# Storing the falling tiles by way of device memory, and another order in the last pair of an attention and Fourier-mixing kernel

## The chip, the cores and the metric

The kernel runs on one core of a Trainium2 chip. The core has a matrix engine (TensorE, PE in the profile), a vector engine (VectorE, DVE), a scalar engine (ScalarE, ACT), a general engine (GpSimd, POOL) and a fifth that here only issues transfers (SyncE, SP). Each runs its own list of instructions in order and waits on semaphores for the others. Transfers between device memory and the core's on-chip memory (SBUF) are carried by 16 DMA engines, called lanes here. SyncE or ScalarE issues a transfer; its pieces then queue in the lanes, and each lane that takes part reports its landing on a semaphore.

The metric is the device time of one execution, in microseconds (us). Three executions of the kernel before took 1045.64, 1046.65 and 1047.59 us; the median is 1046.65.

## The reference

There are 4 batches of 768 tokens, 8 heads of 64 columns. First comes block-sparse attention, with a mask over blocks of 32 tokens, then a Fourier mixing layer with a two-layer network:

```python
scores = where(mask, q @ k.T / 8, -1e9)
x = softmax(scores) @ v                 # 4 x 768 x 512 after the heads are joined
u = x + real(fft2(x))                   # along tokens and along columns
un = (u - mean(u)) / sqrt(var(u) + 1e-6)
out = u + relu(un @ w_ch1) @ w_ch2      # 512 -> 2048 -> 512
```

All inputs and the output are float32.

## The kernel before

The attention of the four batches runs in 96 slots of some 6 to 8 us. A slot computes scores for two tiles of keys (`scores`, L583), exponentials on ScalarE (`weigh`, L603 and L611), the mask on VectorE (L613) and products with v (`values`, L657). Beside the attention of batch b, the kernel carries out the mixing of batch b-1 in the gaps that a planner inside the program finds with estimated costs. The order of the instructions on every engine is fixed when the program is built. After the last slot only the mixing of batch 3 is left, from some 790 us on.

A batch's 768 tokens do not lie in SBUF in their order in memory. The Fourier transform along the tokens is folded by symmetries, and so the 768 rows are kept in six tiles of 128 partitions, three in `xA` (tiles 0, 1, 2) and three in `xB` (tiles 3, 4, 5). The table `_ORDER` says which rows a tile holds, as (tile, first partition, runs, jump, count, first row, step). Tiles 0, 1 and 5 rise: partition after partition holds every second row upwards. In tiles 2, 3 and 4 the partitions 1 to 126 hold rows that fall by two, as two interleaved runs (tile 2: 382, 380, ... and 383, 381, ...), and partitions 0 and 127 hold a row each apart.

`_rows` turns this table into transfers. A rising tile is stored by two transfers of 64 rows (tile 5 by four). A falling tile is stored by three: one row, then 2 x 63 rows in one transfer whose outermost dimension has size 2, then one row. `store` (L1289) issues them, all on SyncE except where the caller names ScalarE. Stores of batches 0, 1 and 2 are called from `channels` (L1279) once the last quarter of the second layer has been added to x (L1284).

The buffers `xA` and `xB` exist twice. The attention output of batch b is therefore copied (`place`, L681, on ScalarE) into the buffer that batch b-2 is stored from, and must wait until those stores have read it. Copies of pair 0 of batches 2 and 3 are placed after the program has emitted batch b-2's stores for that half (`until`).

Between the normalisation and the first layer, rows and columns of `un` must be swapped. For batches 0, 1 and 2 VectorE transposes blocks of 32 x 32 in place (L1019), SyncE writes the tile to device memory (`far<-un`, L1020), and when all three tiles of a half have landed, SyncE gathers them back with the blocks in swapped order (`unT<-far`, four transfers, L1032). All this stands in SyncE's one list, together with the loads of the next pairs' q, k and v (`qb`, `kb`, `vr`) and the output rows of the attention (`row<-oT`, `x<-row`).

In batch 3 the second layer is done by `outputs` (L1335) as seven block products for each pair of tiles (m of xA and m of xB): seven products of four accumulating steps (L1349) take the place of eight, with sums and differences on VectorE (L1356, L1379, L1332). The pairs come in the order `OUT`, 0, 1, 2. After the last pair, tiles 2 and 5, nothing is left but their stores. They are issued by halves of 256 columns: `ends` marks the pair. The last thing stored is the right half of falling tile 2.

At the end of the program there is a branch over a general path that is taken only for large inputs, and closing waits for all transfers.

Of the kernel before, what the change touches and what calls it, by code (L numbers as in the profile page):

```python
# [11 lines left out]
FP32 = mybir.dt.float32  # L12
# [5 lines left out]
ALU = mybir.AluOpType  # L18
# [22 lines left out]
def _grid(ap, start, runs, jump, n, step):  # L41
# [17 lines left out]


_TURNED = (((0, 0, (128, 64, 2), (64, 128, 2), (1, 1, 64)),
# [39 lines left out]
def kernel(  # L101
# [14 lines left out]
    nc = tc.nc  # L116

    B, H, S, D = q.shape
    DM = H * D
    FF = w_ch1.shape[1]  # L120
    P = 128
# [9 lines left out]
    T = C // 2  # L131
# [55 lines left out]
    far_p = ctx.enter_context(tc.tile_pool(name="far_p", bufs=1, space=bass.MemoryType.DRAM))  # L187
    ps_s = ctx.enter_context(tc.tile_pool(name="ps_s", bufs=2, space=PSUM))
# [793 lines left out]
    z_at = [0.0, 0.0]  # L982
    rstd_at = deque()
    finished = set()
    folded = set()

    def mixer(b, xA, xB):
# [298 lines left out]
            if r == NF // 4 - 1:  # L1286
                store(half, m)

        def store(half, m, cols=slice(0, DM), queue=nc.sync):  # L1289
            x = (xA, xB)[half]  # L1290
            for p0, cnt, rows in _rows(out[b][:, cols], T * half + m):
                queue.dma_start(out=rows, in_=x[p0:p0 + cnt, m, cols])
            if cols.stop == DM:
                stored[half] += 1
            if stored[half] == T:
                finished.add((b, half))

        stored = [0, 0]
        last = b == B - 1
        OUT = (0, 1, 2) if last else (2, 0, 1)
        out_of = (OUT, OUT if last else (0, 1, 2))
        o_t, o_s = {}, {}
        DH = DM // 2
# [1 line left out]
        def block(r, k, n):  # L1308
            return w2_sb[:, 8 * r + 4 * k:8 * r + 4 * k + 4, n * DH:n * DH + DH]
# [25 lines left out]
        def outputs(r, m, after):  # L1335

            if m == OUT[0]:
                output_left(m, 1)
                output_left(m, 2)
            a11, a12, a21, a22 = (hs[g, i][:, :, m * P:(m + 1) * P]  # L1340
                                  for i in range(2) for g in range(2))
            a0, a1 = xA[:, m, 0:DH], xA[:, m, DH:DM]
            b0, b1 = xB[:, m, 0:DH], xB[:, m, DH:DM]
            rights = {j: [o_t[j, 0], o_t[j, 1]] for j in (1, 2, 3, 4)}

            def product(pool, tag, a, c):
                ps = pool.tile([P, 512], FP32, tag=tag, name="yy")[:, 0:DH]
                for k in range(4):
                    nc.tensor.matmul(ps, a[:, k, :],  # L1349
                                     c[k // 2][:, k % 2, :] if isinstance(c, list) else c[:, k, :],  # L1350
                                     start=(k == 0), stop=(k == 3))
                busy("PE", 1.75)
                return ps

            def plus(to, a, c=None):
                tt(out=to, in0=a, in1=to if c is None else c, op=ALU.add)  # L1356
                busy("DVE", 0.43)

            def ahead(j):
                if after is not None:  # L1360
                    output_left(after, j)

            ends = r == 1 and after is None
            u = sum_p.tile([P, DH], FP32, tag="oT", name="u")
            p1 = product(ps_m, "m", a11, block(r, 0, 0))
            nc.scalar.copy(out=u, in_=p1)
            plus(a0, p1)
            plus(a0, product(ps_m, "m", a12, block(r, 1, 0)))
            if ends:
                store(0, m, slice(0, DH))  # L1370
            if m == OUT[0]:
                output_left(m, 3)
                output_left(m, 4)
            plus(u, product(ps_t, "t", a21, rights[2]), u)
            plus(a1, u)
            plus(b0, product(ps_s, "s", a22, rights[4]))
            plus(u, product(ps_s, "s", o_s[m, 3], rights[3]), u)
            both = xB[:, m, :].rearrange("p (n d) -> p n d", n=2)
            tt(out=both, in0=both,  # L1379
               in1=u.rearrange("p (o d) -> p o d", o=1).broadcast_to([P, 2, DH]), op=ALU.add)  # L1380
            busy("DVE", 0.7)


            if ends:
                store(1, m, slice(0, DH), nc.scalar)
            p5 = product(ps_o, "o", o_s[m, 1], rights[1])
            plus(b1, p5)
            if r == 1:
                store(1, m, slice(DH if ends else 0, DM))
            plus(a1, p5)  # L1390
            ahead(1)
            ahead(2)
            ahead(3)
            p3 = product(ps_m, "m", o_s[m, 4], block(r, 1, 1))
            plus(a1, p3)
            if r == 1:
                store(0, m, slice(DH if ends else 0, DM))
            ahead(4)

        fl = [[("tm"[h == 1 and m != 0], lambda h=h, m=m: un_flip(h, m), 0.6, 0.55, 0.0)  # L1400
# [29 lines left out]
        for r in range(0 if last else NF // 4):  # L1430
# [21 lines left out]
    needed = set()  # L1452
    state = {"paired": False, "total": None, "w": 0, "got": 0, "owed": 0.0, "ready": 0.0,
             "back": 0.0, "place": None,
             "alone": False, "drain": lambda: None}

    def channel_step():
        masks["by_pe"] = False
# [97 lines left out]
    def w_loads():  # L1556
        while state["got"] < min(len(wchunks), state["w"] + len(W_ROOMS)):
            w_load(state["got"])
            state["got"] += 1

    def w_steps(sl):
        while state["w"] < min(len(wchunks), W_PACE * sl):
            w_round(state["w"])
            state["w"] += 1

    def slot(sl):
        phase, r = divmod(sl, SB)
        n, s = divmod(sl, SP)
        units = range(SLOT * sl, SLOT * sl + SLOT)
# [122 lines left out]
        while short and (not more or soon) and (  # L1692
# [5 lines left out]
            short.remove(item)  # L1698
            item[2]()
        w_loads()  # L1700
        w_steps(sl)
        table_step(sl)

# [32 lines left out]
    begin(B - 1)  # L1736
    state["drain"] = lambda: None
    until(lambda: len(finished) == 2 * B, True)
    ordered.close()

    def general():
# [4 lines left out]
        for b in range(B):  # L1748
# [52 lines left out]
                step[1]()  # L1801
            for fn, _ in rest:
                fn()

    with tc.If(over > 0):
        general()
# [37 lines left out]
```

## Time and profile before

| what | us |
|---|---|
| median of three executions | 1046.65 |
| profiled execution | 1045.29 |
| its span, first to last instruction | 1043.6 |
| TensorE busy | 1018.6 |
| VectorE busy | 683.2 |
| ScalarE busy | 359.3 |
| GpSimd busy | 257.7 |
| ScalarE's copy into x, longest wait (L681) | 8.7 |
| last add of the last pair, start | 1035.50 |

The profile's page gives shares of busy time for the whole span, and for 40 slices of 26.1 us. The granted clock is the share of TensorE's full clock that the chip allowed; its mean is 0.994. A row of the timeline gives the start of a group of instructions, its time, the engine, the line in the kernel, and in brackets how long the engine had been idle before and what released it. The releaser is inferred from semaphore events: where an instruction waits for several things, the one named is that whose event came last by the profile, which need not be the one that mattered. Rows of SyncE's queue (SPq) give the time that issuing took, not the time of the transfer.

### The profile page before, as it was taken

Reading aid. Unit: us, or ns where it says so; the run is one execution under the profiler, and the core shown is the slowest. Engines: PE = TensorE matmul, PEld = TensorE weight load, DVE = VectorE, ACT = ScalarE, POOL = GpSimd, SP = SyncE. Lnnn points to the kernel's source line nnn. Section 1 sums busy time; section 2 is a strip of 40 time slices with the busy share of each in tenths; the row PEclk is TensorE's granted clock in tenths of the full one; section 3 lists DMA queues with packets and bytes.
Section 4 is the critical chain, followed back from the end, with each engine's and each line's share of the span. In section 5 each row is a group of like instructions: output and inputs, shape, how many; then the busy total and the mean of one; then the engine's idle time right before and its main releaser. Section 6 shows DMA issues by size and latency. Waiting matters only on the chain.

```text
span 1043.6 us, 12498 instructions
## 1 busy us (share of the span) xinstructions
PE 1018.6 (98%) x4382; PEld 537.0 (51%) x4382; DVE 683.2 (65%) x1246; ACT 359.3 (34%) x727; POOL 257.7 (25%) x287
## 2 busy tenths in 40 slices
PE   8999999999999999999999998999999999999996
PEld 4444345435565454444535653444444764578575
DVE  6899895978745646655677367665458475674663
ACT  6998765563021012433341111253220221210210
POOL 1000173662000203545560003256540221000000
PEclk9999999999999999999999999899999999999998
DMA  7767422291000143322320005521010001000001
GB/s 213 225 190 234 99 47 46 51 153 25 1 1 20 41 58 65 73 47 45 63 46 1 1 20 101 91 48 43 17 23 8 0 1 42 20 0 1 1 19 45
DMA packets 163582, 58.06 MB, mean 56 GB/s; under 512 B 144298, under 2 KB 154296, under 8 KB 163512
## 3 DMA queue, kind: packets, MB, share of 16 engines
q1 hardware_dynamic: 162216, 56.46, 24.1%
q10 hardware_dynamic: 1264, 0.72, 0.3%
q8 instruction: 36, 0.59, 0.2%
q14 instruction: 34, 0.28, 0.1%
q0 software_dynamic: 32, 0.01, 0.0%
HBM read 43.80 MB, written 13.37 MB: 55 GB/s over the span
## 4 chain that ended last, share of the span: by engine, by line
PE 84%; DVE 8%; DMA 2%; ACT 2%; SPq 2%; issue 1%; ACTq 0%; DVEq 0%
PE y L1281 20%; PE z L1116 16%; PE s L583 11%; PE o L657 9%; PE yp L1116 8%; PE yy L1349 7%; PE xp L1116 4%; PE zp L865 2%; PE sp L728 1%; PE s L593 1%; DMA far<-un 1%; ACT e L603 1%; DVE t L1070 1%; PE yz L1224 1%; DVE acc L638 1%
## 5 line engine op out<-in xcount | busy, mean ns | idle before, releaser
L643 POOL TENSOR_TENSOR acc<-acc,e 128x384 f32<-128x384 f32 x160 | 163.4, 1054 | 126.3 <-DVE e L613 106.7
L583 PE MATMUL s<-qT,kT 64*128 64x384 f32 x768 | 154.5, 518 | 9.5 <-DVE e L613 5.4
L657 PE MATMUL o<-e,vr 128*64 128x384 f32 x768 | 141.7, 497 | 0.0
L1281 PE MATMUL y<-w_sb,hB 128*128 128x512 f32 x264 | 118.9, 601 | 0.0
L1281 PE MATMUL y<-w_sb,hA 128*128 128x512 f32 x264 | 117.1, 595 | 0.0
L613 DVE TENSOR_TENSOR e<-s,mask 128x768 f32<-128x768 f32 x86 | 78.3, 950 | 53.9 <-ACT s L611 45.9
L583 PEld LDWEIGHTS s<-qT,kT 64*128 64x128 f32 x768 | 64.4, 187 | 90.0 <-ACT e L603 22.7
L1284 DVE TENSOR_TENSOR x<-y,x 128x512 f32<-128x512 f32 x66 | 45.6, 691 | 98.3 <-PE y L1281 98.1
L611 ACT ACTIVATE s<-s 128x768 f32<-128x768 f32 x86 | 65.1, 791 | 107.3 <-PE s L583 107.2
L603 ACT ACTIVATE e<-s 128x768 f32<-128x768 f32 x106 | 81.0, 814 | 54.2 <-PE s L593 32.9
L643 POOL TENSOR_TENSOR acc<-e 128x384 f32<-128x384 f32 x42 | 48.7, 1180 | 201.5 <-ACT e L603 121.9
L1116 PE MATMUL z<-unT,t 128*128 128x384 f32 x256 | 93.1, 486 | 0.0
L657 PEld LDWEIGHTS o<-e,vr 128*64 128x64 f32 x768 | 47.9, 136 | 69.4 <-issue 67.0
L1281 PEld LDWEIGHTS y<-w_sb,hB 128*128 128x128 f32 x264 | 49.6, 192 | 62.0 <-issue 61.3
L1121 DVE TENSOR_TENSOR hA<-z,hA 128x384 f32<-128x384 f32 x64 | 35.7, 557 | 69.8 <-PE z L1116 69.7
L1281 PEld LDWEIGHTS y<-w_sb,hA 128*128 128x128 f32 x264 | 49.2, 190 | 59.5 <-issue 55.7
L1125 ACT ACTIVATE hA<-hA 128x384 f32<-128x384 f32 x64 | 33.5, 523 | 121.8 <-DVE hA L1121 121.8
L1116 PEld LDWEIGHTS z<-unT,t 128*128 128x128 f32 x256 | 48.6, 190 | 34.1 <-DVE hA L1121 0.4
L1125 ACT ACTIVATE hB<-hB 128x384 f32<-128x384 f32 x64 | 33.5, 523 | 86.0 <-DVE hB L1121 86.0
L1136 ACT COPY hA<-xp 128x384 f32<-128x384 f32 x32 | 15.3, 477 | 129.3 <-PE xp L1116 129.3
L1116 PE MATMUL z<-t,w_sb 128*128 128x384 f32 x128 | 46.7, 487 | 1.5 <-DVE t L1070 1.5
L1116 PE MATMUL xp<-unT,w_sb 128*128 128x384 f32 x128 | 47.2, 492 | 0.0
(236 smaller groups left out, 1440.4 us busy)
## 6 DMA issues: line engine op xcount, KB each, us to landing
wraw<-in_moe_w_ch_dram SPq DMA_DIRECT2D x32, 512.0 KB
vr<-in_v_dram SPq DMA_DIRECT2D x30, 192.0 KB
far<-un SPq DMA_DIRECT2D x18, 256.0 KB
unT<-far SPq DMA_DIRECT2D x24, 192.0 KB
qb<-in_q_dram SPq DMA_DIRECT2D x44, 96.0 KB
kb<-in_k_dram SPq DMA_DIRECT2D x44, 96.0 KB
out_dram<-x SPq DMA_DIRECT2D x11, 252.0 KB
out_dram<-x SPq DMA_DIRECT2D x19, 128.0 KB
```

Source lines behind the costliest of these rows:

```text
L583: nc.tensor.matmul(s[:, i, 0:HS], kT[rows, c * P:(c + 1) * P], qT[rows, queries], start=True, stop=u not in by_pe)
L603: nc.scalar.activation(out=e, in_=s[:, :, 0:HS], func=ACT.Exp, scale=scale)
L611: nc.scalar.activation(out=s[:, :, 0:HS], in_=s[:, :, 0:HS], func=ACT.Exp, scale=scale)
L613: nc.vector.tensor_tensor(out=e, in0=s[:, :, 0:HS], in1=m.broadcast_to([P, 2, HS]), op=ALU.mult)
L643: nc.gpsimd.tensor_add(out=acc[:, i, :], in0=start[:, i, :], in1=e[:, i, :])
L657: nc.tensor.matmul(o[D * i:D * i + D, :], vt[:, i, c, :], e[:, i, :], start=(c == 0), stop=(c == C - 1))
L1116: nc.tensor.matmul(to, a[:, k, :], c[:, k, :], start=(k == 0), stop=(k == ND // 2 - 1))
L1121: tt(out=to, in0=ps, in1=a, op=ALU.add)
L1125: nc.scalar.activation(out=h, in_=h, func=ACT.Relu)
L1281: nc.tensor.matmul(y, hs[0, half][:, l, m * P:(m + 1) * P], w2_sb[:, 4 * r + l, :], start=(l == 0), stop=(l == 3))
L1284: nc.vector.tensor_tensor(out=x[:, m, :], in0=y, in1=x[:, m, :], op=ALU.add)
L1349: nc.tensor.matmul(ps, a[:, k, :], c[k // 2][:, k % 2, :] if isinstance(c, list) else c[:, k, :], start=(k == 0), stop=(k == 3))
```

## The change

For batches 0, 1 and 2 a falling tile is no longer stored with a falling pattern from SBUF. `store` first writes the whole tile as it lies, 128 rows of 2 KB, into a scratch tensor in device memory (`falls<-x`), plus, for tiles 2 and 3, the one row of partition 0. Two more transfers per tile, from device memory to device memory, bring the rows into the output in falling order (`out_dram<-falls`). Their pattern has 16 parts of 32 columns (128 bytes) outermost, then 63 or 64 rows with a step of minus two rows, then the 32 columns. These two are not issued at once: they are put into a list (`owed`) with the number of the slot, and at the end of each later slot one is taken from it. What is left is issued before the first store of batch 3.

In batch 3 the tiles are stored from SBUF as before, but single rows come after the longer transfers. The order of the pairs is 2, 0, 1, so the last pair is tiles 1 (rising) and 4 (falling). Its seven products are put in another order: both halves of tile 4 are complete after the fourth and the fifth, both halves of tile 1 after the sixth and the seventh. All stores are issued by SyncE. The arithmetic is the same.

```diff
+_FALLS = {2: ((1, 63, 382), (64, 64, 383)), 3: ((1, 63, 766), (64, 64, 767)),
+          4: ((0, 64, 640), (64, 64, 639))}
...
-        def store(half, m, cols=slice(0, DM), queue=nc.sync):
+        def store(half, m, cols=slice(0, DM), ones=slice(0, DM)):
             x = (xA, xB)[half]
-            for p0, cnt, rows in _rows(out[b][:, cols], T * half + m):
-                queue.dma_start(out=rows, in_=x[p0:p0 + cnt, m, cols])
-            if cols.stop == DM:
-                stored[half] += 1
-            if stored[half] == T:
+            while owed and last:
+                owed.popleft()[1]()
+            falls = T * half + m in _FALLS and not last
+            if falls:
+                turn_round(T * half + m, x[:, m, :])
+            for c, few in ((cols, False), (ones, True)):
+                for p0, cnt, rows in _rows(out[b][:, c], T * half + m) if c else ():
+                    if few == (cnt == 1) and (
+                            not falls or (p0 == 0 and _FALLS[T * half + m][0][0])):
+                        nc.sync.dma_start(out=rows, in_=x[p0:p0 + cnt, m, c])
+            stored[half] += cols.stop - cols.start
+            if stored[half] == T * DM:
                 finished.add((b, half))
+        def turn_round(t, x):
+            rows = far_p.tile([P, DM], FP32, tag=f"fall{t}", name="falls", bufs=2)
+            nc.sync.dma_start(out=rows, in_=x)
+            def fall(p0, n, s0):
+                at, to = rows[p0:p0 + 1, :], out[b][s0:s0 + 1, :]
+                w = DM // 16
+                nc.sync.dma_start(
+                    out=bass.AP(tensor=to.tensor, offset=to.offset,
+                                ap=[[w, 16], [-2 * DM, n], [1, w]]),
+                    in_=bass.AP(tensor=at.tensor, offset=at.offset,
+                                ap=[[w, 16], [DM, n], [1, w]]))
+            for run in _FALLS[t]:
+                owed.append((state["slot"], lambda run=run: fall(*run)))
...
-        OUT = (0, 1, 2) if last else (2, 0, 1)
+        OUT = (2, 0, 1)
...
             p1 = product(ps_m, "m", a11, block(r, 0, 0))
             nc.scalar.copy(out=u, in_=p1)
             plus(a0, p1)
+            if r == 1 and after is None:
+                plus(u, product(ps_t, "t", a21, rights[2]), u)
+                plus(a1, u)
+                plus(u, product(ps_s, "s", o_s[m, 3], rights[3]), u)
+                tt(out=both, in0=both, ...)
+                plus(b0, product(ps_s, "s", a22, rights[4]))
+                store(1, m, slice(0, DH), None)
+                p5 = product(ps_o, "o", o_s[m, 1], rights[1])
+                plus(b1, p5)
+                store(1, m, slice(DH, DM), slice(0, DM))
+                plus(a1, p5)
+                plus(a1, product(ps_m, "m", o_s[m, 4], block(r, 1, 1)))
+                store(0, m, slice(DH, DM))
+                plus(a0, product(ps_m, "m", a12, block(r, 1, 0)))
+                store(0, m, slice(0, DH))
+                return
             plus(a0, product(ps_m, "m", a12, block(r, 1, 0)))
-            if ends:
-                store(0, m, slice(0, DH))
...
-            if ends:
-                store(1, m, slice(0, DH), nc.scalar)
             p5 = product(ps_o, "o", o_s[m, 1], rights[1])
             plus(b1, p5)
             if r == 1:
-                store(1, m, slice(DH if ends else 0, DM))
+                store(1, m)
...
             if r == 1:
-                store(0, m, slice(DH if ends else 0, DM))
+                store(0, m)
...
         w_loads()
+        if owed and owed[0][0] < sl:
+            owed.popleft()[1]()
         w_steps(sl)
```

More of the change, by code (lines that the diff above doesn't have):

```diff
@@ L984 @@
     finished = set()
+    owed = deque()
     folded = set()
@@ L1361, in ahead @@
                     output_left(after, j)
-            ends = r == 1 and after is None
             u = sum_p.tile([P, DH], FP32, tag="oT", name="u")
+            both = xB[:, m, :].rearrange("p (n d) -> p n d", n=2)
             p1 = product(ps_m, "m", a11, block(r, 0, 0))
@@ L1367, in outputs @@
             plus(a0, p1)
+            if r == 1 and after is None:
+                plus(u, product(ps_t, "t", a21, rights[2]), u)
+                plus(a1, u)
+                plus(u, product(ps_s, "s", o_s[m, 3], rights[3]), u)
+                tt(out=both, in0=both,
+                   in1=u.rearrange("p (o d) -> p o d", o=1).broadcast_to([P, 2, DH]), op=ALU.add)
+                busy("DVE", 0.7)
+                plus(b0, product(ps_s, "s", a22, rights[4]))
[9 more added lines that the diff above has]
+                return
             plus(a0, product(ps_m, "m", a12, block(r, 1, 0)))
-            if ends:
-                store(0, m, slice(0, DH))
             if m == OUT[0]:
@@ L1377, in outputs @@
             plus(u, product(ps_s, "s", o_s[m, 3], rights[3]), u)
-            both = xB[:, m, :].rearrange("p (n d) -> p n d", n=2)
             tt(out=both, in0=both,
@@ L1454 @@
              "back": 0.0, "place": None,
-             "alone": False, "drain": lambda: None}
+             "slot": 0, "alone": False, "drain": lambda: None}
     def channel_step():
@@ L1566, in slot @@
     def slot(sl):
+        state["slot"] = sl
         phase, r = divmod(sl, SB)
@@ L1738 @@
     until(lambda: len(finished) == 2 * B, True)
+    assert not owed
     ordered.close()
@@ L1803, in general @@
                 fn()
+            while owed:
+                owed.popleft()[1]()
     with tc.If(over > 0):
```

## The prediction, made before the changed kernel ran

> **What bounds the kernel now.** I read the page first: its busy shares, its 40 slices, its chain.
>
> ```profile
> PE 1018.6 (98%) x4382; PEld 537.0 (51%) x4382; DVE 683.2 (65%) x1246; ACT 359.3 (34%) x727; POOL 257.7 (25%) x287
> ...
> PE   8999999999999999999999998999999999999996
> ...
> PEclk9999999999999999999999999899999999999998
> ```
>
> TensorE is busy 98% of 1043.6 us. Transfers can matter only where TensorE stands still, or where its clock is low. Two slices stick out: the 25th and 26th (626 to 678 us), and the last. So I asked for the waits and the timeline there. First, who waited for whom from 640 to 655 us (engine, line, releaser: us in total, times, longest):
>
> ```profile
> ACT s L611 <- PE s L583: 10.0, 1, 10.0
> ACT x L681 <- DMA far<-un: 8.7, 1, 8.7
> PEld s L583 <- DVE e L613: 6.6, 4, 5.2
> ...
> PE s L583 <- DVE e L613: 4.5, 1, 4.5
> ```
>
> The same view for SyncE's queue, 636 to 650 us, and that queue's timeline:
>
> ```profile
> SPq L1032 <- DMA far<-un: 3.6, 1, 3.6
> ```
>
> ```profile
> 633.06 1.53 SPq L1292 DMA_DIRECT2D out_dram<-x  x3
> 635.09 0.35 SPq L1020 DMA_DIRECT2D far<-un  x1
> 636.49 1.19 SPq L1292 DMA_DIRECT2D out_dram<-x  x2
> 637.79 0.53 SPq L1020 DMA_DIRECT2D far<-un  x1
> 641.98 3.96 SPq L1032 DMA_DIRECT2D unT<-far  x4
> 645.98 1.94 SPq L1292 DMA_DIRECT2D out_dram<-x  x2
> ```
>
> Read it as a chain. At 633.06 the falling tile 2 of batch 1 is stored by three transfers, one of them 2 x 63 rows of 2 KB. The trace's landing events show two landings for that one, at 641.2 and 641.3 (a 128-row transfer shows sixteen): it runs on two DMA lanes. The far<-un of 635.09 uses all lanes. Fourteen landings come early, the last two at 641.92, behind the falling rows. SyncE's gather unT<-far needs all sixteen and stands until 641.98, 3.6 us. Behind it in SyncE's order stand the two stores of tile 1. DVE had finished that tile at 639.9, yet they are issued at 645.98 and land at 650.01. ScalarE's copy into x for batch 3 (line 681) writes the buffer that batch 1 is stored from. It starts at 650.26: the wait that the page puts down to far<-un is one for this store. ScalarE's exponentials, VectorE's masking and the next scores queue behind it (timelines of ScalarE and TensorE):
>
> ```profile
> 650.26 0.48 ACT L681 COPY x<-xt 128x384 f32<-128x384 f32 x1 [8.70 <-DMA far<-un]
> ```
>
> ```profile
> 653.32 2.93 PE L583 MATMUL s<-qT,kT 64*128 64x384 f32 x8 [4.52 <-DVE e L613]
> ```
>
> The busy times by stretch (the last three columns: granted clock, DMA share, GB/s) show the two lanes, 2/16 = 0.125, and what the stall did to the clock:
>
> ```profile
> 641.00:642.00 1.00, 1.00 (x5) 0.52 (x4) 0.10 (x1) 0.56 (x1) 0.00 (x0) 1.00 0.13 51
> ```
>
> ```profile
> 653.30:659.10 5.80, 5.78 (x12) 2.51 (x13) 3.63 (x4) 2.48 (x5) 0.00 (x0) 0.50 1.21 136
> ```
>
> The chain ends like this; TensorE's last product is done at 1035.5, and two lanes are still at work four microseconds later:
>
> ```profile
> 1029.85 5.63 PE yy L1349 x26
> 1035.48 0.02 issue
> 1035.50 0.42 DVE x L1356
> ```
>
> ```profile
> 1039.00:1040.00 1.00, 0.00 (x0) 0.00 (x0) 0.00 (x0) 0.00 (x0) 0.00 (x0) 0.50 0.15 38
> ```
>
> From that add's end (1035.92) to the end of the span are 7.65 us: 0.42 to the issue of the last 2 x 63 transfer (1 KB rows), 5.36 from issue to its last landing at 1041.70, 1.87 of closing waits.
>
> **Part 1, the middle of the run (batch 1's stores).** Removed: the two-lane transfer at 633. In its place stand one 128-row transfer to device memory, of the shape of far<-un (issued 607.90, all sixteen landings by 609.91, 2.0 us), and a one-row store. The two turning transfers come in later slots; by the built order of SyncE's queue tile 2's stand behind both gathers, the first directly ahead of kb. So far<-un of 635.09 lands at about 637.2. The gather is ready as soon as the far<-un of 637.79 is issued, at 638.4 instead of 641.98, 3.6 earlier. I take 3.4, because it now meets the rows of tile 0 (636.49) in the lanes. Tile 1's stores keep their 4.0 us from issue to landing behind the gather, so line 681 starts at about 646.85. TensorE is busy until 648.80 whatever happens, and its scores come 3.06 us after line 681 (653.32 - 650.26): 649.9. Idle is 1.1 instead of 4.5: **3.4 us**. What is late next is the same store, now 1.1 us too late and not 4.5.
>
> The clock: at 0.50 for 5.8 us after the stall. Another TensorE gap, 1.19 us at 668.3, left the granted clock at 1.00 (its stretches in the same view). With 1.1 us of idle I expect no drop, which saves half of 5.8, less 0.2 where the second score would wait for VectorE anyway: **2.7 us**. [...]
>
> Downstream TensorE would run 6.1 us earlier. Do inputs keep up? The second gather waits for far<-un behind tile 1's stores, and moves up with them by 3.4 and more: from its landing at 659.7 to about 656, needed at 666.4 - 6.1 = 660.3. kb (landed 666.9, read at 687.6) and qb (landed 433.4 in batch 0, read at 448.5) have 21 and 15 us. So the 6.1 us stay.
>
> **Part 2, the added transfers.** Per batch there are three first hops and six turning transfers of about 1,000 pieces of 128 bytes, 63 or 64 a lane if on sixteen lanes. No row shows device memory to device memory. Nearest from below: unT<-far reads 128-byte pieces, 96 a lane, landing 1.4 us apart: 15 ns a piece, so 0.9 us a transfer. Nearest from above: row<-oT writes them, 24 a lane, 0.65 us apart: 27 ns, 1.7 us. If read and write add, 2.7 us. I take 1.7, as the write side is the nearer shape. Their issue costs SyncE 0.53 (kb) to 1.2 us (unT<-far under backlog) each. What hides both is the slack above. Each waits at SyncE for its first hop, with kb or qb queued behind; but it stands a slot (some 6 us) later in the order, and a first hop lands in 2.0. On the path: **0**. In their favour, the kb loads, 6.89 us at SyncE behind two-lane rows at 657.8, lose that neighbour. So 0 with -0.3 to +1.0. Batch 0's copy waited 1.9 us (until 400.0) with TensorE busy throughout: 0. Batch 2 stores after 866 us, when SyncE has nothing else: 0.
>
> **Part 3, the last pair.** Seven products stay, in another order. In the old order the second product waited 0.18 us for a PSUM bank (weight load at 1024.83, released by VectorE); now another bank comes second: **0.2 us**. Counted from the last product's end E: the falling half goes out after the fourth and fifth of seven products (1.73 us each) and an add, at E-4.7 and E-3.0. With 63 rows of 1 KB a lane at 46 ns, 2.9 us, and 1.5 us from issue to first row, the two lanes are done with the first at E-0.3, the second at E+2.6, the rising rows behind them at E+3.5, landed E+4.0. The closing 1.87 follows: 5.4 us after the last add instead of 7.65. But SyncE also branches over the unused path. Before, that took from 1037.65 to 1040.15, 2.5 us, and VectorE's branch took 3.7 (1035.51 to 1039.22). SyncE's last issue now ends 1.1 after the add, and 2.1 us of closing work follow the branch: 5.7 with 2.5, 6.9 with 3.7. So the branch is late next. I take 5.8: **1.8 us** (0.7 to 2.2). The last pair's issues, before ten on SyncE and four on ScalarE, are eight on SyncE, so none comes later for that.
>
> Sum: 3.4 + 2.7 + 0 + 0.2 + 1.8 = 8.1 us. The profiled execution took 1045.29 (span 1043.6 and 1.7 around it), 1.36 under the median of 1046.65. From itself the sum gives 1037.2, from the median **1038.5**, which I forecast.
>
> **Rivals.**
> - *The clock drops all the same*, or half of the stall stays: 3.4 + 0.2 + 1.8, 5.4 us, 1041.2. For it: one stall is all there is to read from. Against: the 1.19 us gap without a drop. 0.12.
> - *The middle stays*: the copy at 650.26 waits for something I misread, since the page names far<-un as its releaser. Only 2.0 us of tail: 1044.6. Against: the store's landing at 650.01, and far<-un is no input of that copy. 0.09.
> - *The small pieces are slow*, the other side. Three turning transfers stand between vr and qb, 190 pieces a lane. qb was issued 6.5 us after vr landed and has 15 us more, so it decides from 21.5/190 = 113 ns a piece, four times row<-oT's. At 150 ns qb comes 7 us late in each of batches 0 and 1: 1038.5 + 14 = 1052.5. [...] The rows of row<-oT, 128-byte writes, show nothing of that size. 0.06.
> - *The turning does not spread over sixteen*: on two lanes 504 pieces at 27 ns are 13.6 us a transfer, with x already free; the middle's gain stays. The 21 us of kb's slack cover it: 1038.5, so it shares the forecast's chance.
>
> **How the numbers follow.** The forecast has 0.73. Its own range: from 5.3 (stall of 2 us left) + 0.9 to 7.2 + 2.4 (whole stall gone, tail at its best), 1037.0 to 1040.5 from the median, 1035.7 from the profiled execution. Reaching to the first rival, and 1 us for added transfers, gives 1035.5 to 1042.3, with 0.15 outside. A difference under 0.2%, 2.1 us, can't be told from none. Faster: 0.73 + 0.12 + a third of the second rival, 0.88. Within 0.2%: the rest of it, 0.05, as 2.0 us lies just below. Slower: 0.07, the third rival and a hundredth for what I missed.
>
> **What would show it.** Right: unT<-far at about 638.4, line 681 waiting some 5 us, no 4.5 us gap, PEclk 1.00 from 650 to 660; in the tail no stretch at a DMA share of 0.15 beyond E+4, and waits of SyncE that end near 1039.5. Wrong: the gap still there behind another releaser; a new wait of VectorE or ScalarE for qb, kb or vr; half clock without a long gap; a last landing later than E+5, with the falling half's second transfer as its cause.

## The result, and the profile after

The changed kernel takes 1039.39 us (median; 1039.06 to 1039.66). The kernel before, run beside it on the same chip, took 1046.14. The ratio is 0.9936, with a 95% interval of 0.9923 to 0.9950: 6.7 us less, 5.2 to 8.1. The profiled execution took 1039.66 us, its span is 1037.9.

The page of the kernel after: engines, and TensorE's busy tenths and granted clock in 40 slices.

```profile
PE 1016.1 (98%) x4382; PEld 536.4 (52%) x4382; DVE 683.3 (66%) x1246; ACT 359.5 (35%) x727; POOL 257.8 (25%) x287
...
PE   8999999999999999999999999899999999999996
...
PEclk9999999999999999999999999999999999999999
```

The same 4382 matmuls are 2.5 us less busy (1018.6 before); no slice of PEclk reads 8 any more, where two did, and the mean granted clock is 0.999 instead of 0.994. The dip in the 25th slice is gone; the one left, in the 26th, holds the gap of 1.49 us shown below and the one of 1.30 us before the first layer of batch 1. The last slice still reads 6.

SyncE's queue in the kernel after, 633 to 643 us, then ScalarE's copy and TensorE's scores from the timelines of those engines (start, time, engine, line, and in brackets the idle time before and its releaser):

```profile
633.28 0.32 SPq L1316 DMA_DIRECT2D falls<-x  x1
633.65 0.28 SPq L1305 DMA_DIRECT2D out_dram<-x  x1
635.31 0.32 SPq L1025 DMA_DIRECT2D far<-un  x1
636.72 1.16 SPq L1305 DMA_DIRECT2D out_dram<-x  x2
637.97 0.54 SPq L1025 DMA_DIRECT2D far<-un  x1
638.67 4.16 SPq L1037 DMA_DIRECT2D unT<-far  x4
642.87 2.04 SPq L1305 DMA_DIRECT2D out_dram<-x  x2
```

```profile
647.45 0.48 ACT L685 COPY x<-xt 128x384 f32<-128x384 f32 x1 [5.67 <-DMA far<-un]
```

```profile
650.51 1.78 PE L587 MATMUL s<-qT,kT 64*128 64x384 f32 x8 [1.49 <-DVE e L617]
```

The gather `unT<-far` starts at 638.67 instead of 641.98, and everything behind it follows: tile 1's stores at 642.87 instead of 645.98 (their landing events end at 647.28 instead of 650.01), the copy at 647.45 instead of 650.26, the scores at 650.51 instead of 653.32. The gap is 1.49 us instead of 4.52, and the granted clock is 1.00 in the stretch that follows, where before it was 0.50 from 653.3 to 659.1 us (columns: stretch, length, busy PE, PEld, DVE, ACT, POOL, granted clock, DMA share, GB/s):

```profile
650.00:655.00 5.00, 4.49 (x15) 1.95 (x16) 3.95 (x5) 2.97 (x6) 0.00 (x0) 1.00 1.37 151
```

The two spans can be cut at gaps of TensorE that both kernels have. That tells where the 5.6 us between the profiled executions lie:

| stretch | before, us | after, us | difference |
|---|---|---|---|
| start to the end of the 0.83 us gap at 529.5 | 530.30 | 530.53 | +0.22 |
| from there to the end of the 1.3 us gap before the first layer of batch 1 (669.63, 664.22) | 139.32 | 133.69 | -5.63 |
| from there to the start of the last add | 365.87 | 365.83 | -0.04 |
| last add to the end of the span | 8.07 | 7.90 | -0.17 |
| span | 1043.57 | 1037.95 | -5.62 |

So in these two executions all of it is the middle, and next to nothing the tail. The second row is called "the middle" from here on, and its gain is counted against 139.32. "The tail" is the time from the end of the last add to the end of the span: 7.65 us before, 7.47 after. The transfers themselves end earlier in the tail: the last landing comes 3.90 us behind the last add, and came 5.78 behind it before.

### The profile page after: what moved, and what is told of

The parts are those of the page before. It is cut to its first block, busy times and chain, and to the rows that moved or that the text cites. A ratio compares the mean times of both kernels' runs of the same rounds, so it can differ in the third digit from the quotient of the medians.

```text
span 1037.9 us, 12496 instructions
## 1 busy us (share of the span) xinstructions
PE 1016.1 (98%) x4382; PEld 536.4 (52%) x4382; DVE 683.3 (66%) x1246; ACT 359.5 (35%) x727; POOL 257.8 (25%) x287
## 4 chain that ended last, share of the span: by engine, by line
PE 85%; DVE 8%; ACT 3%; issue 1%; SPq 1%; DMA 1%; ACTq 0%; DVEq 0%
PE y L1286 21%; PE z L1121 16%; PE s L587 11%; PE o L661 10%; PE yp L1121 8%; PE yy L1378 7%; PE xp L1121 4%; PE zp L869 2%; PE sp L732 1%; PE s L597 1%; ACT e L607 1%; DVE t L1075 1%; PE yz L1229 1%; DVE acc L642 1%; PE xt L684 1%
```

## The experiments

**Which half of the change gives the gain.** First only the middle: the falling tiles turned, the last pair and its stores as before. The edit is against the kernel before; `turn_round`, `_FALLS` and the list `owed` are those of the change and are left out here.

```diff
         def store(half, m, cols=slice(0, DM), queue=nc.sync):
             x = (xA, xB)[half]
+            while owed and last:
+                owed.popleft()[1]()
+            falls = T * half + m in _FALLS and not last
+            if falls:
+                turn_round(T * half + m, x[:, m, :])
             for p0, cnt, rows in _rows(out[b][:, cols], T * half + m):
-                queue.dma_start(out=rows, in_=x[p0:p0 + cnt, m, cols])
+                if not falls or (p0 == 0 and _FALLS[T * half + m][0][0]):
+                    queue.dma_start(out=rows, in_=x[p0:p0 + cnt, m, cols])
...
```

> The way through device memory in batches 0, 1 and 2 alone; the last pair as before. If all of the gain is made in the middle of the run, by the stall before the scores at 653 us going from 4.5 to 1.5 us with no half clock after it: 5.2 to 5.7 us faster than before, the time from the last add to the end of the span 7.4 to 7.7 us as before. Rival, the gain is shared with the new last pair: 4 us or less.

Measured: 1041.37 us, ratio 0.9958 (0.9942 to 0.9975), 4.4 us less than before's 1045.84. The interval, 2.6 to 6.1 us, holds the theory's 5.2 as well as the rival's 4, so the times do not decide; the profile says more. The gap before the scores is 0.97 us and the middle gains 6.15. The rest of the profiled run is slower than in the kernel before for two reasons that are taken up below: a granted clock of 0.50 at 883 us, and a tail of 9.54 us, longer than the 7.4 to 7.7 expected.

Then only the tail: the new last pair, no tile turned. The edit is against the kernel after. In this run and the two others below that store a falling tile with the changed `store`, its single rows are issued behind the longer transfer.

```diff
-            falls = T * half + m in _FALLS and not last
+            falls = False
```

> The last pair, the order of pairs and the queue of its stores alone; falling tiles of batches 0, 1 and 2 stored from SBUF by two lanes as before. Theory that SyncE's branch over the unused path and the closing work behind it bound the end: within 0.5 us of before, last add to end of span about 7.4 us. Rival, as I forecast, that the last landing bounds the end: 1.8 us faster, last add to end 5.8 us. The stall of 4.5 us and the half clock after it are there.

Measured: 1043.50 us, ratio 0.9982 (0.9972 to 0.9991): 1.9 us less, 0.9 to 2.9. The middle is untouched (gap 4.95, gain 0.17), the tail is 5.97 us. The theory, drawn from the profiles of before and after, that the new tail is worth at most half a microsecond fell: alone it is worth what the prediction gave it. The two halves add up to 4.4 + 1.9 = 6.3 of the 6.7 us.

**Is it one transfer?** The prediction puts the stall on one store, that of tile 2 of batch 1. So that tile alone is turned, and the eight others and the last pair are left as before (the edit is shown against the run with the middle alone):

```diff
-            falls = T * half + m in _FALLS and not last
+            falls = T * half + m == 2 and b == 1
```

> Only tile 2 of batch 1, one of nine falling tiles, goes through device memory; all else as before. Theory of the two lanes ahead of the gather: the whole middle gain, 5.2 to 5.7 us, with the wait of SyncE for far<-un gone and the scores at about 650.5 us. Rival, that the nine falling tiles share the gain by lighter lanes (loads of k, copies into x): about 1 us.

Measured: 1041.47 us, ratio 0.9957 (0.9941 to 0.9974), as fast as with all nine turned and the old last pair (0.9958). The gather starts at 638.08 and the gap is 1.66 us. But the middle gains 3.81 only. TensorE's timeline and its stretches in this run (columns as above) say why:

```profile
650.09 1.86 PE L586 MATMUL s<-qT,kT 64*128 64x384 f32 x8 [1.66 <-DVE e L616]
```

```profile
650.00:651.70 1.70, 1.61 (x8) 0.60 (x8) 0.90 (x2) 1.61 (x4) 0.00 (x0) 0.99 1.34 190
651.70:655.10 3.40, 3.40 (x6) 1.51 (x5) 2.78 (x3) 0.94 (x2) 0.00 (x0) 0.50 1.48 124
655.10:660.00 4.90, 4.90 (x18) 1.79 (x17) 1.25 (x2) 0.00 (x0) 1.98 (x3) 1.00 0.38 82
```

Here 1.66 us of idle were followed by 3.40 us at a granted clock of 0.50, where the kernel after had 1.49 us and stayed at 1.00. So one tile of nine takes the stall away; whether the clock drops after what is left of it is another matter.

The counterpart turns all tiles but that one:

```diff
-            falls = T * half + m in _FALLS and not last
+            falls = T * half + m in _FALLS and not last and (b, half, m) != (1, 0, 2)
```

> The kernel after, but tile 2 of batch 1 is stored as before, by one 2 x 63-row transfer out of SBUF; the eight other falling tiles are turned in device memory. Theory (that one transfer makes the stall): far<-un lands near 641.9 us again, the gather waits some 3.6 us, line 685 waits over 8 us, TensorE's gap is 4 to 5 us and the clock falls to half; the middle gains under 0.6 us; median 1043.0 to 1044.6, the gain of the last pair alone. Rival (the gain of the middle is spread over several of the nine tiles, or comes from the new places of other transfers): gap under 3 us and median below 1042.

Measured: 1045.29 us, ratio 0.9997 (0.9988 to 1.0006), no difference from before, a little above the 1043.0 to 1044.6 expected. `far<-un` lands at 642.29. SyncE's gather, ScalarE's copy and TensorE's scores:

```profile
642.36 4.00 SPq L1037 DMA_DIRECT2D unT<-far  x4
```

```profile
651.10 0.48 ACT L685 COPY x<-xt 128x384 f32<-128x384 f32 x1 [9.05 <-DMA out_dram<-x]
```

```profile
654.15 2.93 PE L587 MATMUL s<-qT,kT 64*128 64x384 f32 x8 [4.87 <-DVE e L617]
```

The whole stall is back, and so is the low clock (0.53 granted over 653 to 660 us). The middle is 0.51 us slower than before. Here the profile names the store, `out_dram<-x`, as the copy's releaser, where for the same wait it named `far<-un` before and after. Eight turned tiles and the new last pair together are worth nothing that this measurement shows; the tail of this run is one of the long ones (below).

**A smaller dose.** The kernel before, with the two falling runs of tile 2 of batch 1 cut from 63 to 48 rows. This leaves 30 rows of the output of batch 1 unwritten, and the second run's 48 rows are taken from partitions 15 too low.

```diff
+                if cnt == 126 and (b, half, m) == (1, 0, 2):
+                    at = list(rows.ap)
+                    rows = bass.AP(tensor=rows.tensor, offset=rows.offset,
+                                   ap=[list(at[0]), [list(at[1])[0], 48], list(at[2])])
+                    cnt = 2 * 48
```

> The kernel before, with the falling rows of tile 2 of batch 1 cut from 2 x 63 to 2 x 48 in one transfer: 30 rows of the output are left out. It doses the cause: the two lanes are busy 48 x 0.0925 = 4.4 us instead of 5.8. Theory: the gather is issued 1.4 us sooner, at 640.6, the stall is 3.1 us. With the clock still dropping: 1.4 us faster; with no drop at 3.1 us: 1.4 + 2.7 = 4.1 us faster. Rival, that the lanes are not the cause of the wait: no change.

Measured: 1044.71 us, ratio 0.9989 (0.9980 to 0.9999). The gather starts at 640.33, 1.65 us earlier than before; counted from the gap at 529.5 us, which comes 0.33 us earlier in this run, it is 1.30, where 1.4 were expected. The gap is 3.65 instead of 4.52, the clock reads 0.50 over 5.8 us as before, and the middle gains 0.83. The stall followed the length of the two-lane rows (3.65 us of gap with 2 x 48 rows, 4.52 with 2 x 63); the drop of the clock was still there behind 3.65 us of gap, and not behind the 1.49 of the kernel after.

**What is left of the gap.** The prediction names what is late next: the stores of tile 1, behind the gather in SyncE's order. So the gather is moved behind them, in the kernel after:

```diff
-            if half == 1 and len(late) < 2 * T:
+            if half == 1 and len(late) <= T:
                 fetch(0)
```

> The changed kernel with the first gather of batch 2 issued after the stores of tile 1 of batch 1 and one more far<-un; by the built order nothing else moves. Theory, the rest of the stall is that store standing behind the gather in SyncE's order: the copy into x waits about 1 us instead of 5.7, the gap of 1.5 us goes, 1.5 us faster than the changed kernel. Rival, that the copy waits for something else: no change; and if the gather then comes too late for VectorE at 660 us, a loss of some 1 to 3 us there.

Measured: 1037.63 us, ratio 0.9930 (0.9912 to 0.9948). SyncE, ScalarE and TensorE:

```profile
639.92 1.11 SPq L1305 DMA_DIRECT2D out_dram<-x  x2
641.12 0.53 SPq L1025 DMA_DIRECT2D far<-un  x1
641.75 4.23 SPq L1037 DMA_DIRECT2D unT<-far  x4
```

```profile
643.00 0.48 ACT L685 COPY x<-xt 128x384 f32<-128x384 f32 x1 [1.45 <-DMA out_dram<-x]
```

```profile
648.71 1.56 PE L587 MATMUL s<-qT,kT 64*128 64x384 f32 x8
```

The stores go out at 639.92, the copy waits 1.45 us instead of 5.67, and the scores have no idle time in front of them. The middle gains 7.42 us, 1.8 more than the change. The times of the two kernels do not tell them apart (ratios 0.9930 and 0.9936, with intervals that lie over each other); that the rest of the stall is gone is read from the profile.

Then the question turns round: is the way through device memory needed at all, or only SyncE's order? The same one line in the kernel before, with every falling tile stored on two lanes:

```diff
             nc.sync.dma_start(out=lines[half][m], in_=un)      # kernel before
-            if half == 1 and len(late) < 2 * T:
+            if half == 1 and len(late) <= T:
                 fetch(0)
```

> The kernel before, with nothing turned in device memory and the old last pair; only the first gather (unT<-far) stands later in SyncE's list, behind the stores of the batch's remaining tiles. Theory (what held the copy up was the store of tile 1, standing behind a gather that waited for the two-lane rows): the stores of tile 1 are issued near 640 us, as soon as VectorE has finished that tile at 639.9, and land by about 643 though tile 2's falling rows still hold two lanes until 641.3. ScalarE's copy into x is then no longer waited for at 650, TensorE's gap of 4.5 us at 648.8 falls below 0.5 us, the clock stays at 1.00 there, the middle gains 7.0 to 7.5 us; median 1038.0 to 1039.5, as fast as the whole change, without any transfer through device memory. Rival (the two-lane rows must go, since everything issued behind them lands late): the stores of tile 1 land at 646 us or later and the second gather moves past 664 us, a gap of 2 us or more appears there or at the first layer; median above 1042.

Measured: 1039.23 us, ratio 0.9940 (0.9926 to 0.9953), as fast as the whole change. SyncE, ScalarE and TensorE in this run:

```profile
633.25 1.53 SPq L1292 DMA_DIRECT2D out_dram<-x  x3
...
640.11 1.15 SPq L1292 DMA_DIRECT2D out_dram<-x  x2
641.49 0.41 SPq L1020 DMA_DIRECT2D far<-un  x1
642.16 4.70 SPq L1032 DMA_DIRECT2D unT<-far  x4
```

```profile
644.13 0.48 ACT L681 COPY x<-xt 128x384 f32<-128x384 f32 x1 [2.39 <-DMA far<-un]
```

```profile
649.50 1.78 PE L583 MATMUL s<-qT,kT 64*128 64x384 f32 x8 [0.52 <-DVE e L613]
```

The falling rows still hold two lanes until 641.4, and `far<-un` of 635.28 still has its last landings at 642.09. But tile 1's stores are issued at 640.11 and 640.63 and land at 643.72 and 644.04, 3.4 to 3.6 us after their issue. The middle gains 6.59 us, a little less than the 7.0 expected. What cost the time was not the slow transfer by itself, but a queue that stood waiting for it with a store behind it that ScalarE needed.

**The tail and the branch.** Both kernels end with SyncE's branch over the path for large inputs. It is taken out, first of the kernel before, then of the kernel after. These two kernels lack that path, which these inputs never take.

```diff
-    with tc.If(over > 0):
-        general()
```

> The kernel before without the general path for large inputs behind the branch (not taken with these inputs), and so without the branch at the end. Theory: before, both the last landing and the code behind the branch end the run at nearly the same time, so without the branch the landing still holds it: last add to end of span 7.2 to 7.7 us, 0 to 0.4 us faster. Rival, that the landing never mattered: some 2 us faster.

> The changed kernel without the general path and the branch. Theory, the branch binds its end: what is left is the last landing 3.9 us after the last add plus 1.9 us of closing waits, 5.8 us instead of 7.4, so 1.6 us faster than the changed kernel, some 7 us faster than the one before. Rival, the branch is not the bound: last add to end 7.4 us, as in the changed kernel.

Measured: before without the path 1044.56 us, ratio 0.9990 (0.9981 to 1.0000); after without it 1037.01, ratio 0.9922 (0.9905 to 0.9938). The tails are 6.71 us (7.65 with the path) and 4.69 (7.47 with it). The waits of SyncE in the tail, first of the kernel after, then of the same without the path:

```profile
SPq L1851 <- SPq L1851: 2.6, 1, 2.6
```

```profile
SPq L1884 <- DMA out_dram<-x: 1.5, 1, 1.5
```

With the branch SyncE waits for itself, for 2.6 us after the branch of line 1851. Without it, it waits for landings: 1.5 us until the first, 2.60 us behind the last add, then one after the other until the last at 3.68, and the span ends 1.0 us behind that. So in the kernel before the falling rows end the tail (last landing at 5.78 of 7.65 us), and in the kernel after the branch and what follows it do. Both tails came out shorter than expected (7.2 to 7.7, and 5.8): without the path the closing work behind the last landing takes 1.1 and 1.0 us, where the kernel before needs 1.87. By their ratios after without the path and after are not told apart.

If the branch is the bound, an earlier branch helps. The last two stores are handed to ScalarE, so that SyncE branches before the last add is done:

```diff
-                store(0, m, slice(0, DH))
+                store(0, m, slice(0, DH), queue=nc.scalar)
```

> The changed kernel with the very last two stores (left half of tile 1) issued by ScalarE instead of SyncE; the branch is there. Theory: SyncE then branches 1.1 us sooner and the end moves with it, last add to end 6.3 us, 1.1 us faster than the changed kernel. Rival, landing-bound end: no change, as the landings come no sooner.

Measured: 1038.17 us, ratio 0.9931 (0.9914 to 0.9948). SyncE branches 0.47 us before the last add ends instead of 1.19 after it, and the tail is 6.11 us. The branch now costs less than the landings, which end 3.76 us behind the last add. Of the 1.36 us that the tail is shorter than after's, 0.8 are a shorter pause among the closing instructions (taken up below), so the theory's 1.1 us are not all shown to be the branch. The ratio does not differ from after's beyond its interval.

**Both together, and without the turning.** The later gather and ScalarE's last stores in one kernel:

```diff
-            if half == 1 and len(late) < 2 * T:
+            if half == 1 and len(late) <= T:
...
-                store(0, m, slice(0, DH))
+                store(0, m, slice(0, DH), queue=nc.scalar)
```

> The kernel after with two edits: the first gather later in SyncE's list (as in the run where that was done alone, 1037.63) and the last two stores issued by ScalarE. Theory (the gather's place is worth 1.5 to 2 us, SyncE's branch over the unused path 1.3 us of the tail, and the two lie in different stages): no gap before the scores near 649 us, span from the last add's end about 6.1 us instead of 7.5; median 1036.0 to 1036.8. Rival (the tail varies by itself by this much from program to program, and the place of the last issue does not matter): tail 7 us or more, median 1037.4 to 1038.2.

Measured: 1036.25 us, ratio 0.9917 (0.9903 to 0.9930), with a tail of 6.37 us and no gap before the scores: 8.7 us less than the kernel before. The same with all falling tiles on two lanes:

```diff
-            falls = T * half + m in _FALLS and not last
+            falls = False
```

> The kernel with the later gather and the last two stores by ScalarE, but with no falling tile turned in device memory: all falling tiles are stored as before, out of SBUF on two lanes. Theory (with the gather behind tile 1's stores, the two-lane rows hold up nothing that TensorE waits for, so the way through device memory is worth nothing more): line 685 starts at 644 us or earlier, the gap before the scores near 649 us is 0.6 us or less, the middle gains 6.5 to 7.4 us against before, median 1036.0 to 1037.4, within 0.2% of the version that turns. Rival (the two-lane rows cost in other places too, in batches 0 and 2 or at kb's loads behind them, and the later gather only hides one): new gaps of TensorE, and a median of 1038 or above.

Measured: 1037.00 us, ratio 0.9912 (0.9898 to 0.9925). Line 685 starts at 643.83, the gap is 0.35 us, the middle gains 6.77, the tail is 5.85 us. The two intervals lie over each other, so the turning is worth nothing that this measurement can tell once the gather stands later; in the profiles the middle gains 0.64 us less without it, no more than two profiles of an unchanged middle differ (below). No new gap of TensorE shows up in the run without it.

The runs side by side. Gap, middle and tail are from each kernel's one profiled execution. The kernels were timed in several sets, each beside executions of the kernel before, so they are compared by the ratio, not by the median.

| kernel | median | ratio to before | gap before the scores | middle gains | tail | last landing behind the last add |
|---|---|---|---|---|---|---|
| before | 1046.14 | 1 | 4.52 | - | 7.65 | 5.78 |
| after | 1039.39 | 0.9936 | 1.49 | 5.63 | 7.47 | 3.90 |
| middle only | 1041.37 | 0.9958 | 0.97 | 6.15 | 9.54 | 7.13 |
| tail only | 1043.50 | 0.9982 | 4.95 | 0.17 | 5.97 | 3.91 |
| one tile | 1041.47 | 0.9957 | 1.66 | 3.81 | 8.14 | 5.89 |
| 48 rows | 1044.71 | 0.9989 | 3.65 | 0.83 | 9.00 | 7.12 |
| before without the path | 1044.56 | 0.9990 | 5.05 | -0.65 | 6.71 | 5.58 |
| after without the path | 1037.01 | 0.9922 | 1.16 | 5.97 | 4.69 | 3.68 |
| last stores by ScalarE | 1038.17 | 0.9931 | 1.29 | 5.83 | 6.11 | 3.76 |
| gather later | 1037.63 | 0.9930 | none | 7.42 | 7.47 | 3.91 |
| before, gather later | 1039.23 | 0.9940 | 0.52 | 6.59 | 7.77 | 5.97 |
| gather later, ScalarE | 1036.25 | 0.9917 | none | 7.41 | 6.37 | 3.78 |
| all but one tile | 1045.29 | 0.9997 | 4.87 | -0.51 | 7.28 | 3.92 |
| gather later, ScalarE, no turning | 1037.00 | 0.9912 | 0.35 | 6.77 | 5.85 | 3.80 |

The middle of before without the path is that of the kernel before, instruction for instruction, and its reading is -0.65 with a gap of 5.05. So far such a reading can move by itself. The 0.83 of the 48-row run is only a little more, so what that run shows rests on its earlier gather and its shorter gap, not on this column.

## Why the prediction was right, point by point

The forecast of 1038.5 us was 0.9 too low, inside its own range. Some of that is luck, for it is closer than its terms were: from the profiled execution the sum gave 1037.2, and the profiled execution after took 1039.66. Of these 2.5 us, 1.6 are the tail's term, 0.5 the middle's, 0.2 the PSUM bank's, and 0.2 a later start that is in neither kernel's edit. The rest was hidden by chance: the profiled execution of before lay 0.85 us under the median of the runs beside the changed kernel, that of after 0.27 above its own, and the median that the forecast started from was 0.51 above the later one.

**Part 1, the stall: 3.4 us predicted, 3.03 measured** (4.52 - 1.49). The chain was read rightly, link by link. One tile turned took the stall away, all but that one brought it back, a shorter transfer shortened it, and with tile 1's stores ahead of the gather it went without any tile turned. `far<-un` landed at 637.34 (predicted 637.2), the gather started at 638.67 (638.4), the copy at 647.45 (646.85). Of these differences 0.22 are the later start of the whole execution, so the gather came as predicted to 0.05 us. The 0.4 us that are missing come nearly all from tile 1's stores, which took 4.4 us from issue to landing and not 4.0. What the prediction called late next, the same store, was late next: moving it ahead of the gather gave 1.8 us more in the middle.

**The clock: 2.7 us predicted, 2.6 measured** (5.63 - 3.03). The number is right, the ground it stood on is thin. The prediction took the 1.19 us gap without a drop (1.30 in the timeline's row of TensorE) as evidence that 1.1 us of idle are safe. The kernel after had 1.49 us and no drop; the kernel with one tile turned had 1.66 us and a drop. No run was made to find out what divides the two, and the last section has cases that the lengths of the gaps do not divide. The first rival, a drop all the same, was a real possibility with a price of about 1.7 us (3.81 against 5.63, less the 0.17 of the longer gap), and its 0.12 was not too much. The stretch at 0.50 lasted 3.40 us in the run with one tile, behind 1.66 us of idle; in the kernel before, behind 4.52 us, 0.50 was read over 5.8.

**Downstream: the 6.1 us stay.** Right. The stretch from the first layer of batch 1 to the last add is 365.87 us before and 365.83 after, so no input was late.

**Part 2, the added transfers: 0.** Right, and the third rival fell. A turning transfer lands 2.7 to 3.9 us after its issue, and three in a row land at 667.24, 667.96 and 668.92: 0.7 to 1.0 us apart, 11 to 15 ns for each of a lane's 63 or 64 pieces. The prediction took 27 and had 113 as the point from which they would cost. All eighteen show sixteen landings, so the fourth rival is out too. These 128-byte pieces from device memory to device memory took no longer than the 15 ns that the prediction read for those of `unT<-far`; what larger pieces would take on this way no run shows. The kb loads, freed of the two-lane rows, took SyncE 2.77 us instead of 6.89.

**Part 3, the PSUM bank: 0.2.** The stretch up to the last add shrank by 0.04. Nothing of it can be told.

**Part 3, the tail: 1.8 us predicted, 0.18 measured in the profiled pair.** This is the term that failed in the profile of after. The landings did what was said: the last comes 4.3 us after the last product (predicted 4.0), 1.9 earlier behind the last add than before. The branch was named as late next, and took 2.7 us, between the two values given. Then the prediction counted 2.1 us of closing work behind it, and it took 3.6. In the kernel after SyncE has passed all waits for landings 4.55 us behind the last add, and its next instruction comes at 6.07, 1.5 us later, with no semaphore event in the trace that released it. In the run with the tail alone the same two instructions are 0.05 us apart, and its tail of 5.97 us is within 0.2 of the 5.8 predicted. A pause like that is in all but two of the profiles with the new last pair and the branch (0.8 to 1.5 us), and not in the profile of before. So the mechanism was right, and a term was missing that falls to some programs and not to others. The run with the tail alone is 1.9 us faster by its medians; the run with all tiles but one, whose tail has the pause, gains nothing.

The rival "the middle stays" fell with the first run; its doubt about the releaser was fair: the profile's name for that wait is `far<-un` in before, in after and in before with the later gather, and the store in after with the later gather and in the run with all tiles but one.

## What to carry to other kernels

The transfer on two lanes cost little by itself here: with the gather later, the kernels with and without it are not told apart (ratios 0.9912 and 0.9917). It cost where an in-order queue waited for something that shared its lanes and held a needed store behind that wait: 3.6 us at SyncE, and 4.52 us of TensorE behind it. Look first for what stands behind the wait and can go ahead of it: one line of order gave here as much as a new way through memory (0.9940 and 0.9936). Where the profile names a releaser that the waiting instruction does not read, ask which landing ends just before it starts. The tail here had several ends close behind one another (in the kernel after the landings until 3.90 us behind the last add, 2.6 us of waiting at the branch, closing work until 7.47), and what a shorter one was worth was set by the next.

## What the runs showed of the hardware that was not expected

The granted clock fell to half behind much less idle time than the low stretch lasted: in the run with one tile to 0.50 for 3.40 us, behind 1.66 us of idle. Two kernels whose edits lie elsewhere (the middle alone, and the last stores by ScalarE) showed 3.40 us at 0.50 as well, behind the gaps of 1.16 and 0.73 us at 880 us that every kernel has. The stretches of the first of them:

```profile
876.00:882.80 6.80, 4.91 (x24) 2.92 (x23) 3.98 (x9) 1.66 (x3) 1.97 (x4) 1.00 0.27 80
882.90:886.30 3.40, 3.40 (x6) 1.69 (x5) 3.29 (x7) 1.05 (x2) 0.00 (x0) 0.50 1.02 160
886.30:890.00 3.70, 3.70 (x13) 2.24 (x12) 1.38 (x3) 0.30 (x1) 0.00 (x0) 1.00 0.37 58
```

From the gap at 880 us to the last add these two take 149.1 and 149.0 us where the others take 147.8, so such a drop costs 1.2 to 1.3 us.

The lengths of the gaps do not divide these cases from the others. The same two gaps lie in the stretch from 880 to 890 us of the kernel after, and the clock is 1.00 there:

```profile
880.00:890.00 10.00, 7.93 (x34) 4.86 (x33) 7.67 (x16) 2.84 (x6) 0.97 (x2) 1.00 0.60 105
```

It read 1.00 from 850 to 890 us also in the kernel before, with the tail alone, in before with the later gather, with the later gather and ScalarE's stores, and with all tiles but one. Of the gaps before the scores, that of 1.49 us in the kernel after had no drop behind it, and that of 1.66 us in the run with one tile had one; behind 3.65 us (48 rows) and 4.52 us (before) the clock read 0.50 over 5.8 us, longer than the 3.40 behind 1.66. What decides whether the clock drops is not shown; no run was made to test it.

The pause of 0.8 to 1.5 us among SyncE's closing instructions stays open. It comes behind the branch over unused code, at another instruction in different programs. The tail of every kernel with that code has transfers of the kind `instruction` (in after five of 8 KB and one of 16 KB behind the last add), and the two kernels without it have none. Whether the branch's wait, 2.6 us in after, is for them no run shows. They do not settle the pause: one such transfer runs from 4.41 to 4.87 us behind the last add in after, where the pause begins, and one from 4.42 to 4.74 in the run with the tail alone, which has no pause.

In the middle-only and 48-row runs the last landing comes 7.1 us behind the last add with the old last pair, in four others 5.6 to 6.0. In those two SyncE's last 64-row store took 1.66 and 1.60 us to issue where it takes 0.48 before, which moves the falling rows behind it by 1.1 to 1.2. Why it took that long was not tried.
